# Matrix sums of a fused attention and gated feed-forward kernel moved from VectorE to GpSimd, with new seeds for its build-time order

## The chip, the cores and the metric

One core of a Trainium2 chip. The metric is the device time of one execution in microseconds (us), the median of several. The engines are named as in the profile: PE (TensorE; PEld is its weight load), DVE (VectorE), ACT (ScalarE), POOL (GpSimd), SP (SyncE).

## The reference, cut to what matters

Linear attention with cosine weights over 8 batches of 8 heads, 576 positions, 64 columns; its output, as 4608 tokens of 512 columns, goes through a gated feed-forward block of width 1536.

```python
def phi(x, c, s):
    r = np.maximum(x, 0.0)
    return np.concatenate([r * c, r * s], axis=-1)
q_p, k_p = phi(q, cos_w, sin_w), phi(k, cos_w, sin_w)
kv = np.einsum('bhsf,bhsd->bhfd', k_p, v)
z = np.sum(k_p, axis=2)
num = np.einsum('bhsf,bhfd->bhsd', q_p, kv)
den = np.einsum('bhsf,bhf->bhs', q_p, z)[..., None] + 1e-06
x = (num / den)            # regrouped to (4608, 512)
g = x @ w_gate
silu = g * (1.0 / (1.0 + np.exp(-g)))
out = (silu * (x @ w_val)) @ w_out
```

## The kernel before, in words

**Work.** The 4608 tokens are nine groups of 512 (tg 0 to 8). For each group the attention output is normalised (`x`, L822), transposed by DMA (`xT`), multiplied with the gate and val weights, gated into `ht`, and multiplied with the output weights.

**Products with fewer multiplications.** Most of the feed-forward products are done as two by two blocks with seven block products in place of eight (Strassen's scheme in Winograd's form). This needs sums and differences of blocks before the products:

- of the weights, once per kernel: T1 to T4 of the output weights (`fn_t`, L1321, four operations of 128 x 1536 fp16, into `wt_sb`), and W1 to W4 of the gate weights ("G") and of the val weights ("V") (`weight_sums`, L1339, four operations of 128 x 1536 each). The val form is used from group 4 on; before, the val product is plain. T is first used in the output product of group 1.
- of the tokens, for each group: X1 to X4 of `xT` (`x_sum_jobs`, L937, 128 x 512), and S1 to S4 of `ht` (`token_sum_jobs`, L1078). S is formed in two parts, first for blocks 0 and 1 of the width (128 x 1024), then for block 2 (128 x 512). S3 comes first; S1 overwrites a block that S3 reads; S2 needs S1; S4 needs S2.

In before DVE forms all these sums. The block products of gate and val are PE's at L964, the output products at L1127. PSUM has eight banks, which are taken and given back by copies and sums of ACT and DVE (L581, L984, L992, L1000, L1057). DVE also multiplies v by the table (L269) and q by its table (L866).

**Order.** The first 20 us or so are written out by hand (`words`). The rest is a list of jobs that a planner puts in order at build time (`order_once`, L1450). A job names the engines that may do it, with a cost in nanoseconds for each, and the jobs that it comes after. The planner has a clock for each engine; the engine with the earliest clock takes the ready job with the earliest due time (PE: by rank), so a job with two engines goes to whichever is first free for it. Due times and ranks are shifted by a random amount of up to 500 ns (ranks by half of that), from a seed for each 30 us of planned time (`shake`). The jobs are then issued in the order of their planned starts, and each engine executes its own in that order:

```python
for j in sorted(jobs, key=lambda j: j.start):
    j.fn(j)
```

**POOL.** In before its work in the planned part is to issue the loads of the later batches (L117, L122), each batch behind a copy of two elements that waits for an earlier landing (`hold_job`, L836), and the stores of groups 1 to 7 (L1096).

Of the kernel before, what the change touches and what calls it, by code (L numbers as in the profile page):

```python
# [15 lines left out]
ALU = mybir.AluOpType  # L16
# [3 lines left out]
def kernel(  # L20
# [10 lines left out]
    nc = tc.nc  # L31
    B, H, S, D = q.shape
    P = 128
    G = H // 2
# [11 lines left out]
    NTG = NH // GH  # L46
# [504 lines left out]
    def d2(n):  # L551
        return 70 + n / 1.92 + PAD

    def d4(n):
        return 73 + n / 3.84 + PAD

    def sc(n, sbuf=False):
        return 69 + n / 1.2 + (27 if sbuf else 0) + PAD

# [29 lines left out]
    def relu_on(eng, out, in_):  # L589
        relu_op("act" if eng == "ACT" else "dve", out, in_)  # L590

    J_ = {}
    LOADED = {("k", 1): 0.0, ("v0", 1): 5700.0, ("v1", 1): 7100.0, ("q0", 0): 1600.0, ("q0", 1): 9400.0, ("q1", 1): 17800.0,
              ("q", 2): 20600.0}
    WO_AT = (11900.0, 14400.0, 17000.0)
# [331 lines left out]
    def xs_of(tg):  # L927
        return xs_more if tg == NTG - 1 else xs_sb

    def x_sum_jobs(tg):  # L930
        t = [J_.get(("xT", 4 * tg + i)) for i in range(4)]
        own = tg == NTG - 1
        old = {} if own else J_.get(("x", tg - 1), {})

        def sum_job(n, x, y, after):
            def fn(j):
                tt(out=xs_of(tg)[:, n - 1], in0=x(), in1=y(), op=ALU.subtract)  # L937
            before = [J_["kvmm", B - 1]] + J_["weighed", B - 2] if own else J_.get(("xs_free", tg - 1, n), J_["kvd_free"])
            return Job({"DVE": d2(512)}, fn, after=after + before + [old[k] for k in ("X2", "X4") if k in old])
        Bs = [lambda i=i: x_parts(tg)[i] for i in range(4)]  # L940
        x3 = sum_job(3, Bs[3], Bs[1], t)
        x1 = sum_job(1, Bs[1], Bs[0], t)
        x2 = sum_job(2, Bs[3], lambda: xs_of(tg)[:, 0], t + [x1])
        x4 = sum_job(4, Bs[2], lambda: xs_of(tg)[:, 1], t + [x2])
        J_.setdefault(("xT_read", tg), []).extend([x1, x2, x3, x4])
        J_["x", tg] = dict(X1=x1, X2=x2, X3=x3, X4=x4)
# [119 lines left out]
    def token_sum_jobs(tg):  # L1066
        last = {}
        free = {1: [], 2: [], 3: [], 4: []}
        if tg > 1:
            p = J_["products", tg - 1]  # L1070
            free = {3: p["P7"], 1: [], 2: p["P6"] + J_["ts", tg - 1][4], 4: p["P3"]}
        res = {n: [] for n in (1, 2, 3, 4)}
        for us, lo, hi in (((0, 1), 0, 4), ((2,), 4, 6)):
            n_el = (hi - lo) * HT

            def s(n, o, x, y, op, after):
                def fn(j):
                    tt(out=o[:, lo_:hi_], in0=x[:, lo_:hi_], in1=y[:, lo_:hi_], op=op)  # L1078
                lo_, hi_ = lo, hi
                jb = Job({"DVE": d2(n_el)}, fn, after=after + free[n])  # L1080
                res[n].append(jb)
                return jb
            s3 = s(3, S3, aq[:, 0, 0], aq[:, 0, 1], ALU.subtract, blocks_of(tg, 0, 0, us) + blocks_of(tg, 0, 1, us))
            s1 = s(1, S1, aq[:, 0, 1], aq[:, 1, 1], ALU.add, [s3] + blocks_of(tg, 1, 1, us))
            s2 = s(2, S2, S1, aq[:, 0, 0], ALU.subtract, [s1])
            s(4, S4, aq[:, 1, 0], S2, ALU.subtract, [s2] + blocks_of(tg, 1, 0, us))
        J_["ts", tg] = res
        return res
# [227 lines left out]
    def fn_t(n):  # L1316
        o, x, y = ((T1, bq[:, 0, 1], bq[:, 0, 0]), (T2, bq[:, 1, 1], T1), (T3, bq[:, 1, 1], bq[:, 0, 1]),
                   (T4, bq[:, 1, 0], T2))[n]

        def fn(j):  # L1320
            tt(out=o, in0=x, in1=y, op=ALU.subtract)  # L1321
        return fn
    WSUM_AT = {"G": 30000.0, "V": 40000.0}
    TSUM_AT = 30000.0

    tsum = []
    for n in (0, 1, 2, 3):
        tsum.append(Job({"DVE": d2(1536)}, fn_t(n), after=tsum, rel=TSUM_AT))
    J_["tsum"] = tsum

    def weight_sums(which, w4, free, over):

        W1, W2, W3, W4 = ws_of[which]
        A11, A12, A21, A22 = w4[:, 1, 0], w4[:, 1, 1], w4[:, 0, 0], w4[:, 0, 1]
        prev = []
        for n, o, x, y, op in ((3, W3, A11, A21, ALU.subtract), (2, W2, A22, W3, ALU.subtract), (4, W4, A12, W2, ALU.subtract),
                               (1, W1, A21, A22, ALU.add)):
            def fn(j, o=o, x=x, y=y, op=op):
                tt(out=o, in0=x, in1=y, op=op)  # L1339
            prev.append(Job({"DVE": d2(1536)}, fn, after=(over if n == 1 else free[n]) + prev,  # L1340
                            rel=WSUM_AT[which] if n != 1 else 0.0))
        J_["wsum", which] = prev

# [103 lines left out]
    def occ(j):  # L1447
        return min(j.engs.values())

    def order_once(nominal):  # L1450
        succ = {j: [] for j in jobs}
        for j in jobs:
            for d in j.after:
# [36 lines left out]
        order_of = {j: n for n, j in enumerate(jobs)}  # L1490

        def shake(j):
            seed = SEEDS[min(len(SEEDS) - 1, int(est[j] / 30000.0))]
            return random.Random(100003 * seed + order_of[j]).uniform(-SHAKE, SHAKE) if seed else 0.0
        for j in topo:
            if "PE" not in j.engs:
# [37 lines left out]
                learn(j)  # L1534
        n_left = len(jobs)
        horizon = 0
        while n_left:
            e = min(at, key=lambda e: at[e])
            t = at[e]
            if e == "PE":  # L1540
                while pe_left and pe_left[0].start is not None:
                    pe_left.pop(0)
            cands = []
            for j in known[e]:
                ra = rooms_at(j)
                if ra is None:
                    continue
                if e == "PE" and j is not pe_left[0]:
                    if rank_of[j] > rank_of[pe_left[0]] + AHEAD:
                        continue  # L1550
                    if j.get and sum(f[0] <= t for f in free["bank"]) - sum(r.n for r in j.get if r.kind == "bank") < RESERVE:
                        continue
                cands.append((max(est0[j], ra), j))
            now_ = [c for c in cands if c[0] <= t]
            pick = None
            if now_:
                rank = (lambda c: rank_of[c[1]]) if e == "PE" else (lambda c: due[c[1]])
                for c in sorted(now_, key=rank):
                    j = c[1]
                    end = t + j.engs[e]  # L1560
                    late = max(0.0, at["PE"] - rank_of[pe_left[0]]) if pe_left else 0.0
                    if e in ("ACT", "DVE") and any(
                            a < end and due[u] + late < end and due[u] < due[j] and a - t < WAIT for a, u in cands if a > t):
                        continue
                    pick = j
                    break
            if pick is None:
                later = [c[0] for c in cands if c[0] > t] + [x for k, x in at.items() if x > t]
                at[e] = min(later + [t + 20.0])
                if t > 1e6:  # L1570
                    raise AssertionError(("stuck", n_left, [j.key for j in pe_left[:4]], free))
                continue
            j = pick
            for k in j.engs:
                known[k].remove(j)
            j.eng, j.start = e, t
            j.done = t + j.engs[e] + (TAIL[e] if j.tail is None else j.tail)
            if j.dma:
                moved[0] = max(t + j.dma[0], moved[0]) + j.dma[1]
                j.done = moved[0] + LATER  # L1580
            at[e] = t + j.engs[e]
            n_left -= 1
            for r in j.get:
                ok = [c for c in choices(r) if c[0] <= t]
                take_ = min(ok, key=lambda c: pleasing(r, c))[1]
                for f in take_:
                    free[r.kind].remove(f)
                r.at = [f[1] for f in take_]
                users[r] = [r.users, 0.0]
                if r.kind == "bank":  # L1590
                    for x in r.at:
                        is_filled[x] = r.fills or r.seeded
            for r in j.put:
                users[r][0] -= 1
                users[r][1] = max(users[r][1], j.done)
                if not users[r][0]:
                    free[r.kind] += [(users[r][1], x) for x in r.at]
            for s, _ in succ[j]:
                missing[s] -= 1
                if not missing[s]:  # L1600
                    learn(s)
        return max(j.done for j in jobs if "PE" in j.engs)

    RESERVE = 1
    LATER = 1500.0
    SEEDS = (69474, 20559, 58306, 34579, 33579, 56752, 69931, 97067, 48890)
    SHAKE = 500.0
    PACK = True
    times, clock = {}, 0.0
    for j in sorted((j for j in jobs if "PE" in j.engs), key=lambda j: j.key):  # L1610
# [1 line left out]
        clock += j.engs["PE"]  # L1612
    ideal = clock
    best = None
    end = order_once(times)
    best = (end,)
    for j in sorted(jobs, key=lambda j: j.start):
        j.fn(j)
# [30 lines left out]
```

## Time and profile before

| | before |
|---|---|
| median of 3 runs | 305.31 us (304.36 to 305.36) |
| the profiled execution: time, span | 305.11 us, 303.3 us |
| PE, DVE, ACT, POOL busy (of the span) | 97%, 82%, 63%, 23% |
| granted clock of PE, mean | 0.998 |
| T sums, V sums on DVE | 4 of 952 ns, 4 of 954 ns in the mean |
| S1, S2, S4 of blocks 0 and 1 on DVE | 24 of some 686 ns |
| S sums of block 2 on DVE | 32 of some 421 ns |

Busy time is from instruction records. A row of the busy table by stretches gives the stretch, its length, then the busy microseconds and instruction counts of PE, PEld, DVE, ACT and POOL, the granted clock, the share of the DMA engines and GB/s. A row of a timeline or of the chain gives the start, the time, the engine, the line and what is written and read. A group row ends with busy time, the mean of one in ns, and the idle time before them.

### The profile page before, as it was taken

To read this page: it belongs to the slowest core of one execution; us is meant where nothing else is said; L and a number is where in the kernel's file an instruction comes from. 1 tells how busy PE (TensorE), PEld (TensorE's weight loads), DVE (VectorE), ACT (ScalarE), POOL (GpSimd) and SP (SyncE) were. 2 spreads that over 40 slices of the span, in tenths; PEclk is the share of its full clock that TensorE was granted. 3 is DMA by queue.
4 is the path that set the end of the run, shared out by engine and by line. 5 is a ranking of instruction groups with operands and counts; after the bars stand their busy time and mean duration, and the time that the engine had idled before them with its cause. 6 is when DMAs were issued, how large, how long until landed. Compare 5 with 4: busy or idle time off the path is not lost. (4 is left out here: it accounts for less than half of the span.)

```text
span 303.3 us, 7733 instructions
## 1 busy us (share of the span) xinstructions
PE 294.4 (97%) x3097; PEld 228.3 (75%) x3097; DVE 249.1 (82%) x506; ACT 191.4 (63%) x389; POOL 71.3 (23%) x125
## 2 busy tenths in 40 slices
PE   8799999999999999999999999999999999999993
PEld 4487455445786678766888888888888888888873
DVE  7875758699999997899879996999679968885792
ACT  8465466945775675964778599956575565744720
POOL 7854302001208034411250204100500050005000
PEclk9999999999999999999999999999999999999999
DMA  7999997987799999998999744960540053005005
GB/s 267 224 197 197 205 204 107 234 183 113 111 213 194 192 179 147 198 263 136 161 205 202 113 78 80 191 99 2 117 94 0 20 109 85 2 0 131 9 14 126
DMA packets 72339, 41.00 MB, mean 135 GB/s; under 512 B 49264, under 2 KB 69232, under 8 KB 72304
## 3 DMA queue, kind: packets, MB, share of 16 engines
q0 software_dynamic: 24976, 24.91, 48.5%
q1 hardware_dynamic: 46880, 15.21, 26.0%
q8 instruction: 24, 0.39, 0.5%
q10 hardware_dynamic: 448, 0.39, 0.4%
q14 instruction: 11, 0.09, 0.1%
HBM read 37.75 MB, written 9.44 MB: 156 GB/s over the span
## 5 line engine op out<-in xcount | busy, mean ns | idle before, releaser
L1096 POOL DMA_DIRECT2D out_dram<-ob x56 | 29.4, 533 | 118.1 <-ACT ob L583 79.7
L1023 ACT ACTIVATE sg<-banks 128x512 bf16<-128x512 f32 x63 | 36.0, 601 | 8.9 <-PE banks L964 8.7
L1127 PEld LDWEIGHTS <-ht 128*128 128x128 f16 x384 | 37.1, 98 | 5.6 <-issue 0.4
L964 PEld LDWEIGHTS <-wg_sb 128*128 128x128 f16 x336 | 32.4, 98 | 6.6 <-issue 0.5
L581 ACT COPY banks<-banks 128x512 f32<-128x512 f32 (+1 forms) x45 | 25.2, 570 | 15.9 <-PE banks L964 6.6
L964 PEld LDWEIGHTS <-wgs_sb 128*128 128x128 f16 x312 | 30.3, 98 | 4.5
L984 DVE TENSOR_TENSOR banks<-m,banks 128x512 f32<-128x512 f32 x36 | 24.6, 693 | 7.9 <-ACT m L581 6.1
L583 ACT ACTIVATE ob<-banks 128x512 f32<-128x512 f32 x34 | 20.1, 599 | 17.1 <-PE banks L1127 15.4
L1127 PEld LDWEIGHTS <-sums 128*128 128x128 f16 x288 | 27.8, 98 | 4.0 <-DVE sums L1078 0.9
L1057 DVE TENSOR_TENSOR ht<-sg,banks 128x512 f16<-128x512 bf16 x45 | 30.3, 681 | 0.0
L964 PE MATMUL banks<-kvt,wgs_sb 128*128 128x256 f16 x192 | 27.2, 273 | 0.0
L964 PEld LDWEIGHTS <-wv_sb 128*128 128x128 f16 x240 | 23.3, 98 | 4.3 <-issue 1.3
L1127 PE MATMUL banks<-wo_sb,ht 128*128 128x256 f16 x192 | 25.5, 273 | 0.0
L964 PE MATMUL banks<-xT,wg_sb 128*128 128x256 f16 x168 | 25.2, 273 | 0.0
L581 ACT COPY m<-banks 128x512 f32<-128x512 f32 x36 | 21.0, 593 | 6.5 <-PE banks L964 6.1
L1127 PE MATMUL banks<-wt_sb,sums 128*128 128x256 f16 x192 | 24.2, 273 | 0.6 <-DVE sums L1078 0.6
L1039 PE MATMUL banks<-xT,wv_sb 128*128 128x512 f16 x96 | 23.8, 379 | 0.0
L1127 PE MATMUL banks<-wt_sb,ht 128*128 128x256 f16 x192 | 22.9, 273 | 0.0
L1023 ACT ACTIVATE sg<-m 128x512 bf16<-128x512 f32 x21 | 13.3, 634 | 15.2 <-DVE m L992 15.2
L964 PE MATMUL banks<-kvt,wg_sb 128*128 128x256 f16 x144 | 19.8, 273 | 0.2 <-DVE banks L984 0.2
L269 DVE TENSOR_TENSOR v<-raw_kv,tab 128x1152 bf16<-128x1152 bf16 x27 | 19.3, 752 | 0.3 <-ACT raw_kv L445 0.3
L822 DVE TENSOR_TENSOR x<-banks,rec 128x512 f16<-128x512 f32 x27 | 18.0, 686 | 1.0
(156 smaller groups left out, 584.2 us busy)
## 6 DMA issues: line engine op xcount, KB each, us to landing
out_dram<-ob POOLq DMA_DIRECT2D x56, 128.0 KB, 3.5
raw_kv<-in_k_dram POOLq DMA_DIRECT2D x7, 576.0 KB, 6.9
raw_q<-in_q_dram POOLq DMA_DIRECT2D x12, 288.0 KB, 8.7
raw_kv<-in_v_dram POOLq DMA_DIRECT2D x6, 576.0 KB, 9.2
wo_sb<-in_moe_w_out_dram POOLq DMA_DIRECT2D x3, 512.0 KB, 12.8
out_dram<-ob SPq DMA_DIRECT2D x12, 128.0 KB, 3.8
wg_sb<-in_moe_w_gate_dram POOLq DMA_DIRECT2D x5, 256.0 KB, 9.0
wv_sb<-in_moe_w_val_dram POOLq DMA_DIRECT2D x5, 256.0 KB, 9.6
```

What stands on the lines that cost most here:

```text
L269: nc.vector.tensor_tensor(out=v2s[b == 1][:, g, :, :, 0:D], in0=(first if b == 0 and g == 0 else {"v": raw_of(b, "v")})["v"][:, g].unsquee ...
L581: nc.scalar.copy(out=out, in_=in_)
L583: nc.scalar.mul(out=out, in_=in_, mul=mul)
L822: tt(out=one(x_all, x).rearrange("p (y e d) -> p e y d", e=2, d=D), in0=view()[:, :, :, 0:D], in1=rec_all[:, t % 4].rearrange("p (e y) o - ...
L964: nc.tensor.matmul(out=to[:, i], lhsT=a[:, c, 2 * u + i], rhs=x()[:, :, c], start=first and i == 0 and c == 0, stop=c == KH - 1, skip_grou ...
L984: tt(out=bank(c), in0=one(m7_all, m).rearrange("p i x -> p (i x)"), in1=bank(b), op=ALU.add)
L1023: nc.scalar.activation(out=gates(rooms[w])[:, :, jh * HT:(jh + 1) * HT], in_=src, func=AF.Silu, scale=DOWN)
L1039: nc.tensor.matmul(out=bank(v), lhsT=wv_sb[:, kc, fc * P:(fc + 1) * P], rhs=xT[tg][:, :, kc], start=(kc == 0), stop=(kc == KC - 1))
L1057: tt(out=ht[:, 4 * u + w:4 * u + w + 3:2, jh * HT:(jh + 1) * HT], in0=gates(rooms[w])[:, :, jh * HT:(jh + 1) * HT], in1=src.rearrange("p ( ...
L1096: {"POOL": nc.gpsimd, "SP": nc.sync, "ACT": nc.scalar}[j.eng].dma_start(out=out_v[idx // NC, idx % NC][:, cols], in_=ob_of(t)[e * SH:(e + ...
L1127: nc.tensor.matmul(out=to, lhsT=a[:, kc, i * P:(i + 1) * P], rhs=b[:, kc], start=first and kc == 0 and i == 0, stop=kc == HC - 1, skip_gro ...
```

## The change

- The four T sums and the four V sums may be done by POOL only; the planner is given 250 + 2.3 n ns for n columns.
- S1, S2 and S4 of blocks 0 and 1 may be done by DVE or POOL, in all groups. S3, the sums of block 2, the G sums and the X sums stay on DVE.
- The seeds of the order's shifts are new and hold for 10 us each in place of 30.
- `order_once` takes the seeds as an argument and can stop early; it is called once with all of them and doesn't stop early.

```diff
+    def gp(n):
+        return 250 + 2.3 * n
+
+    def either(n):
+        return {"DVE": d2(n), "POOL": gp(n)}
+
+    def engine(j):
+        return nc.gpsimd if j.eng == "POOL" else nc.vector
...
+    T_ON = {"POOL": gp(1536)}
+    W_ON = {"G": {"DVE": d2(1536)}, "V": {"POOL": gp(1536)}}
+    X_ON = {"DVE": d2(512)}
+    S_POOL = (1, 2, 4)
+    S_GROUPS = range(NTG)
...
         def sum_job(n, x, y, after):
             def fn(j):
-                tt(out=xs_of(tg)[:, n - 1], in0=x(), in1=y(), op=ALU.subtract)
+                engine(j).tensor_tensor(out=xs_of(tg)[:, n - 1], in0=x(), in1=y(), op=ALU.subtract)
...
-            return Job({"DVE": d2(512)}, fn, after=after + before + [old[k] for k in ("X2", "X4") if k in old])
+            return Job(X_ON, fn, after=after + before + [old[k] for k in ("X2", "X4") if k in old])
...
             def s(n, o, x, y, op, after):
                 def fn(j):
-                    tt(out=o[:, lo_:hi_], in0=x[:, lo_:hi_], in1=y[:, lo_:hi_], op=op)
+                    engine(j).tensor_tensor(out=o[:, lo_:hi_], in0=x[:, lo_:hi_], in1=y[:, lo_:hi_], op=op)
                 lo_, hi_ = lo, hi
-                jb = Job({"DVE": d2(n_el)}, fn, after=after + free[n])
+                jb = Job(either(n_el) if n in S_POOL and not lo and tg in S_GROUPS else {"DVE": d2(n_el)}, fn, after=after + free[n])
...
         def fn(j):
-            tt(out=o, in0=x, in1=y, op=ALU.subtract)
+            engine(j).tensor_tensor(out=o, in0=x, in1=y, op=ALU.subtract)
...
-        tsum.append(Job({"DVE": d2(1536)}, fn_t(n), after=tsum, rel=TSUM_AT))
+        tsum.append(Job(T_ON, fn_t(n), after=tsum, rel=TSUM_AT))
...
             def fn(j, o=o, x=x, y=y, op=op):
-                tt(out=o, in0=x, in1=y, op=op)
-            prev.append(Job({"DVE": d2(1536)}, fn, after=(over if n == 1 else free[n]) + prev,
+                engine(j).tensor_tensor(out=o, in0=x, in1=y, op=op)
+            prev.append(Job(W_ON[which], fn, after=(over if n == 1 else free[n]) + prev,
...
-            seed = SEEDS[min(len(SEEDS) - 1, int(est[j] / 30000.0))]
+            seed = seeds[min(len(seeds) - 1, int(est[j] / WINDOW))]
...
-    SEEDS = (69474, 20559, 58306, 34579, 33579, 56752, 69931, 97067, 48890)
+    SEEDS = (12303, 1207, 1207, 13108, 4526, 14147, 14147, 14147, 14147, 14147, 45145, 66862, 66862, 91102, 74048, 74048, 80233, 5296, 44414, 17741, 72126, 5246, 41217, 78194, 98735, 98735, 2671, 2671, 2671)
     SHAKE = 500.0
+    WINDOW = 10000.0
```

More of the change, by code (lines that the diff above doesn't have):

```diff
@@ L1448, in occ, with order_once @@
         return min(j.engs.values())
-    def order_once(nominal):
+    def order_once(nominal, seeds, until=1e9):
         succ = {j: [] for j in jobs}
@@ L1536, in order_once @@
         horizon = 0
-        while n_left:
+        while n_left and at["PE"] < until:
             e = min(at, key=lambda e: at[e])
@@ L1601, in order_once @@
                     learn(s)
-        return max(j.done for j in jobs if "PE" in j.engs)
+        return max(j.done for j in jobs if "PE" in j.engs and j.start is not None)
     RESERVE = 1
     LATER = 1500.0
-    SEEDS = (69474, 20559, 58306, 34579, 33579, 56752, 69931, 97067, 48890)
+    SEEDS = (12303, 1207, 1207, 13108, 4526, 14147, 14147, 14147, 14147, 14147, 45145, 66862, 66862, 91102, 74048, 74048, 80233, 5296, 44414, 17741, 72126, 5246, 41217, 78194, 98735, 98735, 2671, 2671, 2671)
     SHAKE = 500.0
+    WINDOW = 10000.0
     PACK = True
@@ L1614 @@
     best = None
-    end = order_once(times)
+    end = order_once(times, SEEDS)
     best = (end,)
```

## The prediction

> **What bounds the kernel now.** I read the page first, busy time and the chain that ended last:
>
> ```profile
> PE 294.4 (97%) x3097; PEld 228.3 (75%) x3097; DVE 249.1 (82%) x506; ACT 191.4 (63%) x389; POOL 71.3 (23%) x125
> PE 32%; DVE 2%; DMA 2%; issue 1%; ACT 0%; DVEq 0%
> ```
>
> PE is the bound: of the 37% of the span that the chain covers it holds 32. POOL is three quarters idle, DVE is not. What the change can win is the time in which PE waits for DVE, so next the busy table by stretches (columns: PE, PEld, DVE, ACT, POOL, granted clock, DMA), from the first sum that the change moves to the last matmul:
>
> ```profile
> 58.00:78.00 20.00, 20.00 (x181) 9.92 (x180) 19.39 (x35) 11.18 (x25) 1.74 (x5) 1.00 0.80 152
> 78.00:96.00 18.00, 18.00 (x221) 14.87 (x220) 17.92 (x34) 13.50 (x27) 5.67 (x11) 1.00 1.11 192
> 96.00:142.00 46.00, 46.00 (x446) 32.99 (x445) 41.70 (x81) 30.64 (x61) 14.29 (x21) 1.00 1.12 191
> 142.00:182.00 40.00, 39.84 (x458) 35.14 (x457) 35.70 (x69) 30.65 (x64) 8.91 (x16) 1.00 0.81 144
> 182.00:212.00 30.00, 29.53 (x416) 25.70 (x415) 25.37 (x48) 23.53 (x54) 4.21 (x8) 1.00 0.53 94
> 212.00:243.00 31.00, 31.00 (x313) 27.49 (x311) 25.28 (x51) 17.58 (x35) 4.17 (x8) 1.00 0.27 57
> 243.00:272.00 29.00, 28.66 (x274) 25.44 (x273) 23.35 (x45) 17.24 (x33) 4.17 (x8) 1.00 0.24 51
> 272.00:298.70 26.70, 26.09 (x236) 22.74 (x234) 19.38 (x37) 10.99 (x21) 4.17 (x8) 1.00 0.23 57
> ```
>
> The clock is full. PE is idle for 0.16 + 0.47 + 0.34 + 0.61 = 1.58 us in 240.7. DVE has almost no room up to 96 us (0.61 and 0.08 us idle) and 4 to 8 us in each later row. The chain in order of time says what ended PE's stops:
>
> ```profile
> 189.16 0.62 DVE v L269
> 189.78 0.61 DVE x L822
> 190.43 12.19 PE banks L964 x108
> ...
> 290.42 0.45 issue
> 290.86 0.43 DVE sums L1078
> 291.34 3.23 PE banks L1127 x28
> ```
>
> One 0.62 us multiply in front of an urgent one on DVE was enough to stop PE near 190 us, and near 291 us it was a token sum that came late. The 0.34 us in the row 243 to 272 belongs to a landing of xT, which the change leaves alone. So DVE's part is at most 1.58 - 0.34 = 1.24 us.
>
> **The change, part by part: what DVE is rid of.** The four weight sums T take 0.952 us each and the four V sums 0.954; S1, S2 and S4 of blocks 0 and 1 take 0.686 each, in 8 token groups, if the planner gives all 24 to POOL. That is 3.8 + 3.8 + 16.5 = 24.1 us of DVE. Worth for PE: between nothing and 1.24 us; I take half, **-0.6**, because the stop near 190 us is behind a v multiply, which stays.
>
> **What POOL does instead.** No row shows a two-input tensor operation on POOL. The nearest ones:
>
> ```profile
> L174 POOL MEMSET kvt<- 128x520 f32 x1 | 0.5, 531 | 0.0
> masks.py:199 POOL TENSOR_SCALAR_AFFINE_SELECT ident<-ident 128x128 f16<-128x128 f16 x1 | 0.3, 295 | 0.1
> ```
>
> From below: the memset against a 99 ns one of a single column gives 432 / 519 = 0.83 ns an element, so 0.95 us for 1024 and 1.38 for 1536. From above: the select, which reads, is 2.30 ns an element with its start, so 2.36 and 3.54 us; a second input might double that. I take 2.36 and 3.54, the row that reads (the diff plans with 2.61 and 3.78). POOL then has 4 x 3.54 + 4 x 3.54 + 24 x 2.36 = 85 us more work, 156 of 303: it fits. The price is in latency and in DVE.
>
> The Trainium skill's page "GPSIMD Engine Reference", section 3.1, has 4497 ns for a two-input add of 2048 fp32 columns. By it a sum of 1024 would be an estimated 2.2 us and one of 1536 3.4 us; no row here shows it. The total would hardly change.
>
> **What POOL's reads do to DVE.** One row of before shows both engines at it, in the timelines of POOL and DVE:
>
> ```profile
> 110.77 3.17 POOL L836 CAST hold<-xT 1x2 bf16<-1x2 f16 x1 [11.96 <-DMA xT<-x]
> ...
> 113.93 0.43 DVE L937 TENSOR_TENSOR kvt<-xT,kvt 128x512 f16<-128x512 f16 x1
> ```
>
> A copy of two elements, 0.18 us in its other executions, takes 3.17 us while DVE runs tensor-tensor operations back to back with both inputs in SBUF. It ends at 113.94, just after DVE's first gap (113.90). So these reads exclude each other, at least this way round.
>
> The skill's page "SBUF — State Buffer", section "Who interferes with whom", says it for both ways: a DVE instruction with two SBUF inputs and a GpSimd instruction that reads SBUF share one read interface, and the later one blocks until the other is through. By this rule the change loses DVE time; without it, it would only win. The row agrees for POOL waiting on DVE; none shows DVE waiting on a long POOL read.
>
> I bound it from both sides: no hold at all, or DVE's two-input instruction waits until POOL's ends. Group 7 as an example of the second (DVE's timeline):
>
> ```profile
> 266.58 0.42 DVE L1057 TENSOR_TENSOR ht<-sg 128x512 f16<-128x512 bf16 x1
> ...
> 268.91 0.42 DVE L1078 TENSOR_TENSOR sums<-ht 128x512 f16<-128x512 f16 x1
> ```
>
> S3 starts at 264.65 there and ends at 265.34. With 0.15 us between steps POOL does S1 from 265.49 to 267.85, S2 from 268.0 to 270.36, S4 to 272.9. The multiply of 266.58 (both inputs in SBUF) is held 1.27 us and the sum of 268.91 1.45: 2.7 us, for 2.06 us saved. Laying the same three steps over all eight groups of the trace in this way gives 26.1 us at 2.36 us a sum (7.4 at 0.95). The four T sums, laid from 58.3 us on, hold DVE for 12.0 us (2.1 if short), the four V sums, from 89.2 us on and at 146.6, for 5.3 us.
>
> What of it reaches PE? Where DVE's idle time in the row covers the balance, I take nothing: groups 2 to 8 hold 22.4 us against 14.4 saved and V 5.3 against 3.8, 9.5 us net, and the rows from 96 us on have 32 us idle. Without this cover it would be 9.5 x 0.38 = 3.6 us more, with the rate below. Up to 96 us there is no cover: T 12.0 - 3.8 - 0.6 idle = 7.6 us, and group 1 3.7 - 2.1 = 1.6; 9.2 us. The rate: near 190 us 1.23 us of DVE in the chain (0.62 + 0.61) stand against at most 0.47 us of PE's idle time (row 182 to 212), 0.38. 9.2 x 0.38 = **+3.5**. If reads do not hold DVE this term is 0.
>
> **The last group** has no next group for PE to turn to. S3 of blocks 0 and 1 ends at 288.2; POOL's S1 ends at 290.7 and S2 at 293.3, while before S2 was done at 292.9 just ahead of its product. DVE's own short sums (block 2) are held meanwhile, and S4 comes at 296.4, in time for the last product at 297.2. DVE, rid of S1, gives S3 of block 2 some 0.6 us sooner near 290.9. I take **+0.7** (-0.6 to +2.5, the far end if S4 on POOL gets in ahead of DVE's last sums).
>
> **Queues and waits.** POOL works in order. Behind a T sum stand batch holds and input loads (68.25 and 77.84 us in before); these loads' data land some 7 to 10 us later and batch 3's product starts at 93, so some 6 us of delay are covered, one sum but not two (7.1 us): 0 to 1 us, taken as 0. Stores of a group lie 10 us and more before the next sums: 0. A sum behind a hold waits for that hold's landing, and its output product behind it. V's last sum may start at 141 us, and its first product starts at 154 us: 0.
>
> **The new order.** Other seeds move every job's rank by up to 250 ns on PE and 500 ns elsewhere. It removes and adds no work. Bounds: all of before's 1.58 us won, or as much again lost; I take 0.
>
> **Sum.** -0.6 + 3.5 + 0.7 = +3.6 us. The profiled execution took 305.11 us (span 303.3 and 1.8 around it), 0.2 below the median of 305.31; 305.11 + 3.6 = 308.7 us.
>
> **Rivals.** *Faster:* POOL's reads hardly hold DVE, or find its gaps. For it: both stops that the chain shows end with DVE, and POOL does nothing between a group's stores and the next group's in the later rows. Then -1.24, and -0.6 in the last group: 303.5 us; with the xT stop ordered away, 303.1. Against: the 3.17 us row. *Same:* the holds happen, and DVE's idle time hides them also before 96 us, as T lies elsewhere: within 1.5 us of 305.3. *Slower in another way:* the chain S3, S1, S2, S4 is long, 2 us as DVE work (0.69 each), over 7 on POOL, and products wait for it in each group. It decides if PE has no other ready product within the 5 us; 0.5 us a group for 8 groups give 309. *The change doesn't do what it says:* S may go to either engine and the planner may leave it on DVE; T and V can't. Then only T's term is left, 7.6 x 0.38 = 2.9, less 0.6: 307.6.
>
> **The numbers.** Slower 0.52 (the sum, the long chain and T alone), same 0.20, faster 0.28. The bound is 0.5%, 1.5 us, about what a measurement of this kernel can tell from no change. The range reaches down to the faster case, 303.2. Up: groups 2 to 8 and V uncovered, 308.7 + 3.6, and half of what a delayed load can cost, 0.5: 312.8. The slower case's own range is 306.9 to 312.8.
>
> **What would show it.** POOL rows of two-input sums at 2.2 to 2.7 us (1024) and about 3.5 (1536), 32 of them; DVE's two-input rows (v, the x sums, the short token sums) longer in the mean than the 752, 421 and 421 ns of before, or idle time before them; DVE's share down by less than 24 us; PE idle 2 to 5 us more between 58 and 298 us, most before 96 us. Wrong: DVE's two-input rows keep their means while POOL reads, or PE's idle time falls below 1 us.

## The result, and the profile after

The changed kernel takes 348.64 us (347.47 to 350.9, 4 runs) against 304.88 before (4 runs): 1.1445 times the time, 95% interval 1.1375 to 1.1514. The forecast was slower, but by 3.6 us and not by 44. Its profiled execution took 349.57 us with a span of 347.8, 44.5 more than before. In the changed kernel all line numbers in the planned part are 14 higher than in front (L1078 is L1092). First the page's busy times and chain:

```profile
PE 307.4 (88%) x3097; PEld 232.1 (67%) x3097; DVE 275.8 (79%) x480; ACT 191.0 (55%) x389; POOL 133.2 (38%) x151
PE 60%; DVE 25%; DMA 6%; issue 4%; ACT 3%; SPq 0%; DVEq 0%; ACTq 0%
```

DVE does 26 operations fewer and is busy 26.7 us longer. It has 25% of the chain where it had 2%; the chain covers almost the whole span now and covered 37% of it before. PE is idle for 40.4 us of the span (347.8 - 307.4), 8.9 before: 31.5 us more. The other 13.0 us are in PE's busy time (294.4 before) with the same number of matmuls: they ran slower. The table by stretches shows where, in its clock column (columns as in the prediction):

```profile
50.00:60.00 10.00, 4.60 (x30) 2.23 (x27) 9.72 (x10) 4.12 (x10) 9.52 (x6) 1.00 0.93 178
60.00:70.00 10.00, 8.24 (x30) 3.60 (x31) 5.72 (x10) 5.26 (x11) 1.42 (x1) 0.66 0.49 92
100.00:110.00 10.00, 6.76 (x38) 5.03 (x38) 6.21 (x10) 2.03 (x4) 2.10 (x1) 0.66 0.66 113
200.00:210.00 10.00, 6.06 (x47) 4.67 (x45) 9.78 (x11) 3.11 (x7) 8.30 (x6) 0.88 0.07 11
330.00:343.20 13.20, 9.86 (x76) 7.70 (x73) 9.15 (x13) 1.83 (x4) 4.16 (x2) 0.87 0.15 35
```

Between 50 and 60 us PE works for less than half of the time, while DVE "works" 9.72 us on ten instructions: that is waiting, booked as busy. Just behind it the granted clock is 0.66 in the mean (0.50 from 61 to 67 us). Over the whole span it is 0.965, so (1 - 0.965) x 347.8 = 12.2 us of clock were withheld, which is about the 13.0 us that PE's matmuls took longer.

What the instructions on DVE and POOL cost, in groups by shape (busy us, mean ns, then idle time):

```profile
L1092 DVE TENSOR_TENSOR sums<-ht 128x512 f16<-128x512 f16 x16 | 17.4, 1089 | 0.2
L793 DVE TENSOR_TENSOR x<-numtmp,rec 128x256 f16<-128x256 f32 x10 | 10.2, 1048 | 0.2
L951 DVE TENSOR_TENSOR kvt<-xT,kvt 128x512 f16<-128x512 f16 x12 | 9.0, 747 | 0.1
L782 DVE TENSOR_SCALAR den<-numtmp 128x8 f32<-128x8 f32 x5 | 3.2, 644 | 0.1
...
L1335 POOL TENSOR_TENSOR wt_sb<-wo_sb 128x1536 f16<-128x1536 f16 x2 | 6.2, 3092 | 0.0
L1092 POOL TENSOR_TENSOR sums<-ht 128x1024 f16<-128x1024 f16 x5 | 10.7, 2146 | 0.4
```

The first four had means of 421, 422, 421 and 170 ns, for example in the kernel before:

```profile
L1078 DVE TENSOR_TENSOR sums<-ht 128x512 f16<-128x512 f16 x16 | 6.7, 421 | 0.1
L779 DVE TENSOR_TENSOR x<-numtmp,rec 128x256 f16<-128x256 f32 x10 | 4.0, 422 | 0.2
```

Operations with an input in PSUM kept theirs (for example 679 against 681 ns for `ht<-sg,banks`). Mean after less mean before, times the count, summed over all stretched groups, is **41.6 us of DVE held**. A sum on POOL takes 2.1 to 2.2 us for 1024 columns and 3.1 for 1536 (one of the eight 3.6). The planner gave POOL 18 of the 24 sums S.

The first stretch in detail, timelines of DVE and of POOL:

```profile
51.33 4.11 DVE L793 TENSOR_TENSOR x<-numtmp,rec 128x256 f16<-128x256 f32 x1
55.87 2.54 DVE L782 TENSOR_SCALAR den<-numtmp 128x8 f32<-128x8 f32 x1
...
51.28 0.75 POOL L117 DMA_DIRECT2D raw_kv<-in_v_dram  x1
52.04 3.10 POOL L1335 TENSOR_TENSOR wt_sb<-wo_sb 128x1536 f16<-128x1536 f16 x1
55.22 3.16 POOL L1335 TENSOR_TENSOR wt_sb<-wo_sb,wt_sb 128x1536 f16<-128x1536 f16 x1
```

A multiply of 0.42 us, begun at 51.33, ends at 55.44, 0.3 us after POOL's first sum (55.14). The 0.17 us tensor-scalar of 55.87 ends at 58.41, with the second sum (58.38). PE's transposes wait for this very x: they start at 55.49. A reciprocal of 58.44, inside POOL's third sum, keeps its 0.20 us. PE's waits in the changed kernel (us in total, times, longest):

```profile
PE banks L1141 <- DVE sums L1092: 9.5, 7, 3.3
PE banks L978 <- DVE kvt L951: 7.9, 5, 3.9
PE banks L736 <- DVE x L793: 7.2, 2, 4.0
PE banks L814 <- DVE x L836: 3.3, 1, 3.3
```

These come to 27.9 us, where the same waits came to 0.6 us before; PE's idle time grew by 31.5. In three of the four rows the instruction that PE waits for is itself of the kind that is held.

### The profile page after: what moved, and what is told of

The parts are those of the page before. It is cut to its first block, busy times and chain, and to the rows that moved or that the text cites. A ratio compares the mean times of both kernels' runs of the same rounds, so it can differ in the third digit from the quotient of the medians.

```text
span 347.8 us, 7736 instructions
## 1 busy us (share of the span) xinstructions
PE 307.4 (88%) x3097; PEld 232.1 (67%) x3097; DVE 275.8 (79%) x480; ACT 191.0 (55%) x389; POOL 133.2 (38%) x151
## 4 chain that ended last, share of the span: by engine, by line
PE 60%; DVE 25%; DMA 6%; issue 4%; ACT 3%; SPq 0%; DVEq 0%; ACTq 0%
PE banks L978 23%; PE banks L1141 14%; PE banks L908 8%; DVE sums L1092 5%; DMA phit<-r_q 4%; PE banks L1053 4%; DVE kvt L951 3%; PE banks L424 3%; DVE ht L1071 3%; DVE x L793 2%; DVE ht L1092 2%; PE banks L814 2%; DMA xT<-x 2%; PE banks L697 2%; DVE ht L1060 2%
## 5 line engine op out<-in xcount | busy, mean ns | idle before, releaser
L1141 PEld LDWEIGHTS <-ht 128*128 128x128 f16 x384 | 38.5, 101 | 6.7 <-issue 0.3
L1141 PEld LDWEIGHTS <-sums 128*128 128x128 f16 x288 | 27.9, 100 | 15.9 <-DVE sums L1092 11.8
L1092 POOL TENSOR_TENSOR ht<-ht 128x1024 f16<-128x1024 f16 x6 | 12.8, 2127 | 63.2 <-DVE sums L1092 59.7
L978 PE MATMUL banks<-kvt,wgs_sb 128*128 128x256 f16 x192 | 28.8, 281 | 7.9 <-DVE kvt L951 7.9
L1141 PE MATMUL banks<-wt_sb,sums 128*128 128x256 f16 x192 | 27.1, 285 | 9.6 <-DVE sums L1092 9.5
L998 DVE TENSOR_TENSOR banks<-m,banks 128x512 f32<-128x512 f32 x36 | 24.7, 692 | 11.7 <-PE banks L978 6.8
L1092 DVE TENSOR_TENSOR sums<-ht 128x512 f16<-128x512 f16 (+1 forms) x27 | 27.7, 1030 | 0.4
L1141 PE MATMUL banks<-wo_sb,ht 128*128 128x256 f16 x192 | 27.3, 287 | 0.0
L269 DVE TENSOR_TENSOR v<-raw_kv,tab 128x1152 bf16<-128x1152 bf16 x27 | 20.5, 787 | 0.4 <-ACT raw_kv L445 0.4
L908 PE MATMUL banks<-xT,wg_sb 128*128 128x512 f16 x72 | 20.8, 416 | 0.0
```

The source lines that it names most:

```text
L269: nc.vector.tensor_tensor(out=v2s[b == 1][:, g, :, :, 0:D], in0=(first if b == 0 and g == 0 else {"v": raw_of(b, "v")})["v"][:, g].unsquee ...
L908: nc.tensor.matmul(out=bank(r), lhsT=w[:, kc, fc * P:(fc + 1) * P], rhs=xT[tg][:, :, kc], start=(kc == 0), stop=(kc == KC - 1))
L978: nc.tensor.matmul(out=to[:, i], lhsT=a[:, c, 2 * u + i], rhs=x()[:, :, c], start=first and i == 0 and c == 0, stop=c == KH - 1, skip_grou ...
L998: tt(out=bank(c), in0=one(m7_all, m).rearrange("p i x -> p (i x)"), in1=bank(b), op=ALU.add)
L1092: engine(j).tensor_tensor(out=o[:, lo_:hi_], in0=x[:, lo_:hi_], in1=y[:, lo_:hi_], op=op)
L1141: nc.tensor.matmul(out=to, lhsT=a[:, kc, i * P:(i + 1) * P], rhs=b[:, kc], start=first and kc == 0 and i == 0, stop=kc == HC - 1, skip_gro ...
```

## The experiments

**Theories.** A: POOL's sums, since they read SBUF, hold DVE's instructions that read SBUF through the same port, and PE waits for those. B: the new order is bad by itself. C: the chain S3, S1, S2, S4 is long on POOL and the products wait for it. D: POOL's queue delays loads and holds.

**The order without POOL's sums.** Two kernels: in the first, the changed order stays and DVE executes POOL's sums at their places; in the second, the planner with the new seeds has only DVE for them.

```diff
 def engine(j):                         # order_dve
-    return nc.gpsimd if j.eng == "POOL" else nc.vector
+    return nc.vector
```
```diff
-T_ON = {"POOL": gp(1536)}              # seeds_only
-W_ON = {"G": {"DVE": d2(1536)}, "V": {"POOL": gp(1536)}}
-S_POOL = (1, 2, 4)
+T_ON = {"DVE": d2(1536)}
+W_ON = {"G": {"DVE": d2(1536)}, "V": {"DVE": d2(1536)}}
+S_POOL = ()
```

> The changed kernel with its planned order kept on every other engine, but every sum that was planned for POOL is issued to DVE at its planned place. No POOL sum is left. Theory A (POOL's reads hold DVE's instructions that have two inputs in SBUF, 41 us of held time in the trace of the changed kernel): the holds go, DVE gets about 20 us of sums back in an order that did not plan for them; 304 to 312 us. Theory B (the new order, made by other seeds, is bad by itself): 325 us or more. Theory C (the long chain of sums makes the output products late): the sums take 0.69 us again, so 304 to 312 as in A.

> The new seeds in stretches of 10 us, but the planner may give all sums to DVE only, as in the kernel before. Theory A and C: 303 to 308 us. Theory B: 325 us or more.

Measured: 311.14 us, 1.0207 times before (1.019 to 1.0224), and 307.20 us, 1.009 (1.0063 to 1.0118). B falls as the main cause: the new seeds alone cost some 2.6 us, and the changed order with DVE's sums in it 6.5.

**The same POOL time without reading.** This is the test that tells A from C and D: POOL is as long occupied, at the same places, behind the same waits.

```diff
 def engine(j):
-    return nc.gpsimd if j.eng == "POOL" else nc.vector
+    return write_only if j.eng == "POOL" else nc.vector
+class write_only:
+    def tensor_tensor(out, in0, in1, op):
+        one = (slice(None),) * (len(out.shape) - 1) + (slice(0, 1),)
+        nc.gpsimd.tensor_tensor(out=out[one], in0=in0[one], in1=in1[one], op=op)
+        for _ in range(2):
+            nc.gpsimd.memset(out, 0.0)
```

> The changed kernel with each POOL sum replaced by a sum of one column of each block (so that it waits for the same inputs) and two memsets over the whole output, about 2.2 us for 1024 columns and 3.1 us for 1536: as long, at the same places, with the same waits, but hardly reading. The sums are left out in this way, so the output is not the product. Theory A (reading is what holds DVE): DVE's two-input rows go back to 0.42 and 0.75 us in the mean and the time is 304 to 314 us. Theory C (long chain) and a theory D (POOL's queue delays loads and holds): still 335 to 350 us, with DVE's rows short.

Measured: 305.40 us, 1.0028 times before (1.0014 to 1.0041). POOL is busy for 132.5 us, as in the changed kernel (133.2), in memsets of 951 and 1377 ns, two for each sum. DVE's groups of this kernel (its lines are 8 higher again):

```profile
L1100 DVE TENSOR_TENSOR sums<-ht 128x512 f16<-128x512 f16 x16 | 6.8, 422 | 0.2
L801 DVE TENSOR_TENSOR x<-numtmp,rec 128x256 f16<-128x256 f32 x10 | 4.0, 421 | 0.2
```

The same instructions that took 1089 and 1048 ns are back at 422 and 421, and 43.2 us are gone. One kind is not wholly back: the tensor-scalar `den<-numtmp` has a mean of 404 ns against 170, because one of its five took 1.34 us beside a memset. So writing alone can hold a tensor-scalar; that it holds no two-input operation is what the rows show. C and D fall: chain, queue and order are the same and cost next to nothing. A stands: for the two-input operations it is the reading.

**The port by itself.** Phases in which POOL and DVE are let go together.

```diff
+phases = [(two_in, none), (two_in, long_sum), (one_in, long_sum), (copies, long_sum), (small, long_sum),
+          (two_in, sets), (two_in, lambda: pieces(6)), (two_in, lambda: loads(2)),
+          (two_in, lambda: (loads(2), long_sum())), (lambda: two_in(12), lambda: (loads(1), long_sum())),
+          (none, long_sum), (none, lambda: (loads(2), long_sum()))]
```

> A program of its own, with twelve short phases behind gates: POOL and DVE are let go together. DVE does eight operations of 512 fp16 columns: two inputs in SBUF, or one in SBUF and one in PSUM, or a copy, or a small f32 tensor-scalar; POOL does nothing, one two-input sum of 1536 columns (3.1 us), memsets of the same length, six sums of 256, two loads, or loads and then the sum. It leaves out the whole computation. Theory A: two-input operations wait for the whole sum (one of them 3 us or more), those with a PSUM input keep 0.68 us, memsets hold nothing. In the changed kernel the small f32 tensor-scalar was held too (2.5 us), so I expect it held here, and the fp16 copy held if it uses the same port. Behind two loads the hold should begin while POOL still issues the second load (in the changed kernel DVE was held from 51.3 or 97.8 us, before the sum's recorded start at 52.0 or 99.0): about 3.8 us or more instead of 3.1. A theory that reads share the port would give two-input operations of 0.5 to 0.8 us each and no single long one.

DVE's timeline, eight operations in a row each (of the last phase only the one that is held); without POOL the eight two-input operations of 512 columns take 2.77 us:

```profile
29.44 5.66 DVE L58 TENSOR_TENSOR do<-da,db 128x512 f16<-128x512 f16 x8 [2.51 <-ACT da L53]
37.61 4.87 DVE L62 TENSOR_TENSOR do<-da,bank 128x512 f16<-128x512 f16 x8 [2.50 <-ACT da L53]
44.99 4.59 DVE L66 COPY do<-da 128x512 f16<-128x512 f16 x8 [2.51 <-ACT da L53]
52.54 3.54 DVE L70 TENSOR_SCALAR so<-sm 128x8 f32<-128x8 f32 x8 [2.96 <-ACT sm L54]
59.77 2.77 DVE L58 TENSOR_TENSOR do<-da,db 128x512 f16<-128x512 f16 x8 [3.69 <-ACT da L53]
67.35 5.60 DVE L58 TENSOR_TENSOR do<-da,db 128x512 f16<-128x512 f16 x8 [4.80 <-ACT da L53]
87.71 4.04 DVE L58 TENSOR_TENSOR do<-da,db 128x512 f16<-128x512 f16 x1
```

In order: beside one POOL sum of 3.08 us two-input operations lose 2.9 us, all in one instruction of 3.3 us. With one input in PSUM nothing is lost (0.68 us each). Copies and small tensor-scalars, with a single input in SBUF, are held as well, one of each for 3.2 and 3.0 us. Beside memsets the two-input operations lose nothing; copies and tensor-scalars were not tried beside them. Beside six sums of 256 columns the two engines take turns: 2.8 us lost, 0.47 at a time. In the phase of the last row POOL issues two loads before its sum: one operation, begun at 87.71 during the second issue, took 4.04 us, though the sum's record starts only at 88.35 and is 3.10 long. Behind one load it was 3.97 us. Load issues alone hold nothing (2.77 us for eight).

The Trainium skill's page "SBUF — State Buffer", section "Who interferes with whom", has the two-input rule, adds copies and tensor-scalars in a two-port mode, and exempts a GpSimd instruction that only writes. The rows agree on the first and the last of these for two-input operations, and copies and tensor-scalars are held as it says; that they ran in a two-port mode is what no row shows.

**Part by part.** The new seeds, and one family of sums left for POOL.

```diff
-S_POOL = (1, 2, 4)                     # t_on_pool and v_on_pool
+S_POOL = ()
...
```

The families that do not stay on POOL are planned for DVE by the lines of `seeds_only`.

> Of the changed kernel only the four T sums stay on POOL; V and S are planned for DVE. Theory A, with a rate that the changed kernel suggests (41 us held, 43 us lost, so about 1 us lost for 1 us held in front of what PE waits for): four sums of 3.1 us, of which three to four meet a two-input instruction, 8 to 12 us held, 7 to 13 us over the 307.2 us of the new seeds on DVE: 314 to 320 us. My rate of 0.38 with cover would give 310.

> Only the four V sums stay on POOL. Theory A: three or four holds of up to 3 us, one of them behind load issues and longer; 6 to 12 us over 307.2: 313 to 319 us. If idle time of DVE covers the holds in this stretch (DVE is idle 10% there): 307 to 309.

> Only S1, S2 and S4 of blocks 0 and 1 may go to POOL. In the changed kernel 18 of 24 did, and they held DVE for 22 us in all. Theory A: 18 to 25 us over 307.2: 325 to 332. If DVE's idle time of 10 to 27% from 96 us on covered them, as the prediction had it: 307 to 311.

| sums on POOL | time, us | over 307.2 | DVE held, us |
|---|---|---|---|
| T | 323.84 | 16.6 | 11.1 |
| V | 318.11 | 10.9 | 8.0 |
| S | 331.33 | 24.1 | 24.7 |
| all | 348.64 | 41.4 | 41.6 |

The held time is worked out from group means as above. Each family has two executions; the kernel before took 305.09 us beside them and 304.64 beside the 307.20, so a time over 307.2 is good to about 0.5 us. S alone put 21 of its 24 sums on POOL, not 18. Each family alone is a loss, at 1.0 to 1.5 us for each microsecond held. T came out above what I expected: PE's busy time is 6.2 us longer than with the seeds alone (300.8 against 294.6) at a mean clock of 0.972, and PE waited once 2.9 us for an x sum that waited for a landing of xT, which the seeds alone do not have; so its rate is not that of holds alone. V alone was moved by the planner to meet T's sums on DVE: those took 2104 and 1424 ns in the mean in place of 952.

**The length of a hold.** All POOL sums cut into sums of 256 columns, then only S so cut.

```diff
+class pieces:
+    def tensor_tensor(out, in0, in1, op):
+        for n in range(out.shape[1]):
...
+            nc.gpsimd.tensor_tensor(out=out[at], in0=in0[at], in1=in1[at], op=op)
```

> The changed kernel with every POOL sum cut into sums of 256 columns, nothing else changed. In the program of its own six such sums and DVE's operations took turns, and DVE lost 0.47 us at a time, 2.8 us in all, as much as by one long sum. If what costs is the total held time, the time stays near 345 us. If what costs is the length of one hold against the 0.1 to 0.4 us by which DVE is ahead of PE, and the clock that falls after long stops, it falls to 315 to 330 us, with mean granted clock back at 0.99 or more.

> As the run with only S on POOL (331.3 us, 24 us held), in the same planned order, but each of these sums cut into four of 256 columns. In the run with all sums in pieces a tensor-tensor operation of DVE lost 0.5 us for each piece that it met, but one tensor-scalar waited for 16 pieces in a row (9.8 us), which hid the answer; no tensor-scalar stands in the stretches of S. If the length of a single hold decides, because PE is only some tenths of a us behind DVE, 311 to 320 us. If the total of held time decides, it falls only as far as that total falls: each of 80 or so pieces can hold DVE once for 0.5 us at most, and where DVE has a single two-input operation to do only one piece counts, so some 12 to 16 us held and 319 to 324 us.

The first took 331.0 us in its profiled execution and 344.1 in its other one, too far apart to decide between the two expectations. Its trace has a few long holds (timelines of DVE and POOL):

```profile
52.48 9.99 DVE L790 TENSOR_SCALAR den<-numtmp 128x8 f32<-128x8 f32 x1
90.99 3.58 DVE L1100 TENSOR_TENSOR sums<-ht 128x512 f16<-128x512 f16 x1
...
51.79 3.79 POOL L569 TENSOR_TENSOR wt_sb<-wo_sb 128x256 f16<-128x256 f16 x6
55.54 3.78 POOL L569 TENSOR_TENSOR wt_sb<-wo_sb,wt_sb 128x256 f16<-128x256 f16 x6
59.29 3.78 POOL L569 TENSOR_TENSOR wt_sb<-wo_sb 128x256 f16<-128x256 f16 x6
```

A tensor-scalar on eight columns waited for 16 short sums in a row. Two-input tensor-tensors mostly got in after one short sum (0.92 us in place of 0.42), but not always: one took 3.58 us and another 3.16, each beside a row of them. What decides between the two is open. S in pieces took 316.67 us, 1.0423 times before (1.038 to 1.0466): 14.7 us less than S whole. All of its holds but one (2.5 us) are of at most 0.5 us. Held time fell by 8.1 us, from 24.7 to 16.6, the loss over the seeds by 14.6, from 24.1 to 9.5, so a microsecond held costs 0.6 and no longer 1.0, and the mean clock is 0.999 in place of 0.990. Both matter, the total and the length of each hold.

**Is it the order, and what is relief worth?** The old seeds in stretches of 30 us, with POOL's sums and with memsets in their place.

```diff
...
+    SEEDS = (69474, 20559, 58306, 34579, 33579, 56752, 69931, 97067, 48890)
     SHAKE = 500.0
-    WINDOW = 10000.0
+    WINDOW = 30000.0
```

> The changed kernel with the nine old seeds in stretches of 30 us; the sums stay on POOL. Theory A: the loss is the holds', whatever the order: 335 to 360 us. A theory that the new seeds put POOL's sums in an unlucky place: 305 to 325.

> The same with each POOL sum replaced by a sum of one column of each block and two memsets (the sums are left out in this way). It tells what 20 us less on DVE are worth to PE without holds. The prediction's bound was 1.24 us of PE's stops, so at best 303.5 us; with the new seeds the same edit took 305.4. If relief of DVE is worth what the bound says, 303 to 304.5; if new stops take its place, 305 to 308.

Measured: 362.69 us (1.191, 1.1866 to 1.1954) and 311.57 us (1.0226, 1.0189 to 1.0263). The reading costs 51 us in this order, 43 in the other, so the new seeds are not to blame. The second lies above both expectations: 20 us less on DVE bring nothing where the order, planned anew with POOL, makes new stops (x sums behind a landing of xT: 1.6 us; once PE waits 0.9 us for what POOL writes in place of a sum; and others).

## Why the prediction was wrong, point by point

- **Which way:** right. **POOL's sums** at 2.36 and 3.54 us: measured 2.1 to 2.2 and 3.1. Right, a little high. Of the 24 sums S 18 moved.
- **The holds:** right, both that they happen and their total: the long end was 26.1 + 12.0 + 5.3 = 43.4 us, measured 41.6. That the totals agree so well is partly luck: 26 sums moved and not 32, and each held DVE for 1.6 us and not 1.36.
- **What of it reaches PE: this step failed.** It let DVE's idle time in a row (32 us from 96 us on) swallow the balance of held and saved time, and charged only 9.2 us at a rate of 0.38, the term of +3.5. Measured, all of it arrives: 31.5 us more idle time of PE plus 13.0 of slower matmuls, 44.5, for 41.6 held, so 0.76 us of idle time and 0.31 of clock for each microsecond held. S alone, which was to be covered but for one group, lost 24.1 us for 24.7 held. Idle time that stands elsewhere in a row can't be spent on a hold of 1 to 4 us. The held instructions are the x sums, token sums and x, PE's own inputs. The case "groups 2 to 8 and V uncovered", 3.6 us, was priced with the same wrong rate. The rate came from a single stop of some tenths of a microsecond, with PE's idle time divided by the DVE time of the whole chain and not by a delay; it says nothing of a hold of 3 us. S in pieces gives 0.6 with the clock nearly full, whole sums 1.0 and more.
- **The clock** had no term at all. The row 60 to 70 us stands at 0.66 right behind a stretch in which PE worked 4.6 of 10 us; PE's matmuls took 13.0 us longer in all.
- **The last group:** 0.7 us, far end 2.5. Between 330 and 343.2 us PE is idle for 3.3 us, against 0.6 in the last row before, and the clock is 0.87. Both figures were too small.
- **Queues:** 0 to 1 us. Loads as such were not late (with memsets in the queue the time is 305.4), but what stands in front of a sum matters: behind load issues the hold began while the last of them was on record.
- **The new order:** taken as 0 with bounds of 1.58 us either way, measured 2.6.
- **DVE's relief,** at most 1.24 us: with memsets PE is idle for only 0.38 us between 96 us and its last matmul, 1.58 before, so the bound agrees. But a stop of 1.8 us for xT near 81 us took its place, and the time is 305.4, not 303.5. (This trace is of the slowest of ten executions, 306.7 us, so the stop may be shorter in the others.) Thus even sums on POOL that cost DVE nothing would not have beaten the kernel before in this order. The rival "faster" needed that and no holds.
- **The rival of the long chain** gave 309 and is refuted by the same run. **T alone** was given 307.6 and took 323.8, by the same wrong rate.

No version here beats the kernel before.

## What to carry to other kernels

An idle POOL is no free DVE: while one of its sums reads SBUF, the DVE instruction with two inputs there that comes next, or the copy or tensor-scalar, waits for the sum's end (in the program of its own one of each took 3.0 to 3.3 us), and a planner that books the two engines as independent can't see it. Before moving work, list what DVE has to issue within each such sum, and charge PE the whole hold where the held instruction, or the one behind it, feeds PE and arrives only some tenths of a microsecond ahead. A share of idle time over a stretch covers little: S alone lost 24.1 us for 24.7 held. Test a suspected port by replacing the reads with writes of the same length, and see in the rows which kinds of instruction stay long.

## What the runs showed of the hardware that I had not expected

- A hold can begin before the sum that causes it is on record: with POOL's queue at load, load, sum, DVE was held from the second load's issue on, 4.04 us for a sum of 3.10. The loads alone hold nothing. That some of POOL's parts start the sum while others still issue the load is my guess; it may as well be that the record starts late. Neither was tried.
- Back-to-back short sums on POOL mostly let a two-input tensor-tensor in after one of them (0.47 us lost at a time in the program of its own), but a whole row can shut DVE out: a tensor-scalar for 9.99 us, two tensor-tensors for 3.58 and 3.16 us.
- PE's long stops cost a second time. With the stops near 60 and 100 us (4.0 and 3.9 us) the mean granted clock of a 10 us row fell to 0.66; over the whole span 12.2 us of clock were withheld, and PE's busy time is 13.0 us longer. The three stops of 1 to 2 us close together in the row of 200 us (3.9 us idle in all) went with 0.88 in that row and 0.95 in the next. No limit comes out of the rows: behind a stop of 3.1 us at 52 us the clock stayed at 1.00 up to the next stop, and with S alone one of 2.7 us at 190 us was enough (0.83 from 190 to 200 us).
